# Wider opening loads, later second halves and a new order in a fused attention and gated FFN kernel

## The chip, the cores and the metric

The kernel runs on one core of one Trainium2 chip. The metric is device time in microseconds (us) from launch to end. Every change is judged by the median of several runs of the kernel before and after on the same chip.

## The reference

One input `x` of 2048 rows and 512 columns (bf16) goes through two branches, and a gate per row mixes them:

```python
def _A_ref(x, wqkv, wo):                       # sliding window attention
    B, S, D = x.shape
    H = 32; Dh = D // H; W = 256               # 32 heads of 16
    q, k, v = ...(x @ wqkv)...
    scores = einsum("bhqd,bhkd->bhqk", q, k) * (Dh ** -0.5)
    mask = (idx[:, None] - idx[None, :] >= 0) & (idx[:, None] - idx[None, :] < W)
    p = softmax(where(mask, scores, -1e9))
    return einsum("bhqk,bhkd->bhqd", p, v).reshape(B, S, D) @ wo

def _B_ref(x, w1, w3, w2):                     # gated FFN, F = 1376
    return (silu(x @ w1) * (x @ w3)) @ w2

g = sigmoid((x * gate_w).sum(-1, keepdims=True))
return g * a + (1 - g) * b
```

## The kernel before, in words

**Tiling.** The 2048 rows are 16 tiles of 128, or 4 blocks of 512 (`tq`, `tcb`). The 512 columns are 4 groups of 128 (`c`, called channel groups here: 8 heads each). `xT` holds x turned (columns on the partitions). F is cut into 11 pieces `f`: ten of 128 and a last one of 96.

**Attention.** For each `c` and `tq`, `projections` makes K and Q by matmuls of 512 columns (L449) and V (L507); for the very first block K and Q are made in two halves of 256 columns, so that the first half needs only the first two row tiles. `main_batch` (L568) makes scores of one row tile for eight heads into the only PSUM buffer `su`, ScalarE (ACT) takes the exponential of 128x2048 (L572, 1.88 us), and GpSimd (POOL) masks it (L577, L582). `edge_batch` does the same for the window's edges (L618, L622, L635). `pv` multiplies by V (L708), and VectorE (DVE) turns, normalises and turns back into `OT` (L732 to L742). `output` multiplies `OT` by `wo` (L926).

**FFN.** For each block of 512 rows: matmuls with w1 and w3 (L844), tanh on ACT (L854), two products on DVE (L858, L864) into `hT`; the 32 odd columns of F go apart (`tail_columns`, L795) through `hb` and a transposing DMA into `hX` (L819). Then W2 (L897) for four row tiles. For the last row tile (15) W2 runs in three column parts at the very end (`last_part`, L953).

**The order.** All of this is put in a list of jobs by `Plan.add`, with a duration, what it waits for, and a due time. `Plan.emit` walks through a model of the run and writes one fixed order for all engines: the engine that can start first is served, and among its jobs that can start then the one with the earliest due time. Due times come from the constants `K`: attention's batches are spread evenly over `TA` us from `T0` (`at(c, t)`), FFN's work over `TF0` to `TF1`, and offsets (`PV`, `EDGE`, `V`, `LEAD`, `QLEAD`, `PE`, `O0` to `O3` and others) move single kinds. A job of TensorE has a form ("full", "row" for scores, "column" for PV); `ADJ` is taken from the due time of a score or PV job when another has just run, `SEP` is added to a PV job's when a full one has. The order is made when the program is built, so it is fixed; each engine works through its own list and waits by semaphores.

**Loads.** `opening` runs ahead of the plan: a memset, `WARM` small matmuls on zeros (L308), and the first loads, issued on the queues of SP (SyncE) and ACT. x's first four row tiles come as they are into `xs` and are turned by TensorE (L386); the other blocks come by transposing DMA (`turn_x`). `load_w` loads columns f0 to f1 of a weight for all 512 rows, so a row of one transfer is 2 x (f1 - f0) bytes. Weights of Q, K and V come first for group 0 alone; the rest comes by `late`: a small memset on POOL (L361) into the target, planned for a given time, and behind it the load on SP, which must wait for the memset. The lists `landed` tell the plan when each opening load is supposed to be there.

The parts that the change touches, with the line numbers of the profile:

Of the kernel before, what the change touches and what calls it, by code (L numbers as in the profile page):

```python
# [15 lines left out]
P = 128  # L16
# [135 lines left out]
def kernel(  # L152
# [29 lines left out]
    VW = DH + 1  # L182
    HALF = (0, 1, 2, 3, 4)
    SCALE = float(DH) ** -0.5
    WARM = 27

    pp = ctx.enter_context(tc.tile_pool(name="pp", bufs=1))
    ps = ctx.enter_context(tc.tile_pool(name="ps", bufs=1, space=bass.MemoryType.PSUM))
# [41 lines left out]
    su = ps.tile([P, 4, 512], F32, name="su")  # L230
    ch = [ps.tile([P, 512], F32, name=f"ch_{i}") for i in range(4)]

    K = {"T0": 5.549, "TA": 217.14, "TF0": -5.82, "TF1": 246.66, "PV": 1.255, "EDGE": -3.585, "HOLD": -3.739, "LEAD": -1.218, "QLEAD": -5.876, "V": 9.009, "O0": 3.298, "O1": 2.321, "O2": 0.732, "O3": 31.615, "FE": 11.808, "PE": -3.471, "VE": -0.148, "MK": 8.747, "UP": 10.86, "_km": 1.0, "_lo": 1.0, "LE": 6.107, "ADJ": 9.389, "SEP": -24.496, "BE": 0.712, "END": 5.72}
    plan = Plan({"su": 1, "ch": 4, "Em": len(Em), "Ee": len(Ee), "tt": 2, "h1": 2,
                 "tn": len(tn), "ot": len(ot), "hT": 1},
                K["ADJ"], K["SEP"])
# [45 lines left out]
    def load_x(m0, m1, eng):  # L282
        eng.dma_start(out=xs[:, m0:m1, :],
                          in_=x2d[P * m0:P * m1, :].rearrange("(m p) d -> p m d", p=P))
# [6 lines left out]
    def load_w(dst, src, f0, f1, both=False):  # L291

        rows = src[:, f0:f1].rearrange("(c p) f -> p c f", p=P)
        for eng, c0, c1 in ((nc.sync, 0, 2), (nc.scalar, 2, 4)) if both else ((nc.sync, 0, 4),):
            eng.dma_start(out=dst[:, c0:c1, f0:f1], in_=rows[:, c0:c1, :])
# [14 lines left out]
    def opening():  # L310
        nc.vector.memset(warm[:], 0.0)
        constants()
        warm_up(WARM)

        nc.scalar.activation(out=gt[:, 0:4], in_=warm[:, 0:4], func=ACT.Tanh)
        load_x(0, 1, nc.sync)
        load_x(1, 2, nc.scalar)
        load_w(wqkv_sb, A_wqkv, D, D + P, True)
        load_x(2, 3, nc.sync)
        load_x(3, 4, nc.scalar)  # L320
        nc.scalar.dma_start(out=gwr[:], in_=gate_w.rearrange("(c p) -> c p", p=P))
        load_w(wqkv_sb, A_wqkv, 0, P)
        load_w(w1_sb, B_w1, 0, P)
        load_w(w3_sb, B_w3, 0, P)
        load_w(wqkv_sb, A_wqkv, 2 * D, 2 * D + P)
        load_w(w1_sb, B_w1, P, 2 * P)
        load_w(w3_sb, B_w3, P, 2 * P)
        turn_x(1)
        load_w(w1_sb, B_w1, 2 * P, 6 * P)
        load_w(w3_sb, B_w3, 2 * P, 6 * P)  # L330
        turn_x(2, 0, 1)
        load_w(w1_sb, B_w1, 6 * P, F)
        turn_x(2, 1, 2)
        load_w(w3_sb, B_w3, 6 * P, F)
        turn_x(2, 2, 4)
        constants2()
        constants3()
        constants4()
        constants5()
# [3 lines left out]
    PV_DUE, EDGE_DUE, HOLD = K["PV"], K["EDGE"], K["HOLD"]  # L343
    OUT_DUE = [T0 + TA + K["O%d" % i] for i in range(4)]
    step = TA / (NDC * NT)
    landed = {"x": [3.25, 3.4, 4.5, 4.6, 12.2, 21.5], "w13": [6.3, 6.8, 7.9, 8.4, 15.4, 18.7],
              "qkv": [4.1, 5.4, 7.4], "gw": 7.5}

    def at(c, t):
        return T0 + step * (c * NT + t)  # L350
# [17 lines left out]
        return done  # L368

    def rest(b):  # L370
        return lambda: load_w(wqkv_sb, A_wqkv, b * D + P, (b + 1) * D)

    x_in.append(late(25.8, xT[0:1, 0, 3 * 512:3 * 512 + 2], [lambda c=c: turn_x(3, c, c + 1) for c in range(NDC)], 1.27, 2.5))
    for b, us in ((1, 44.6), (0, 46.4), (2, 48.2)):
        qkv_in.append(late(us, wqkv_sb[0:1, 0, b * D + P:b * D + P + 2], [rest(b)]))

    xt_ready = [[] for _ in range(NTC)]
    for m in range(4):
        job = Job()

        def half_bank(job=job):
            return ch[job.at["ch"]][:].bitcast(BF16)[:, 0:D].rearrange("p (c t) -> p c t", c=NDC)

        def tr(m=m, half_bank=half_bank):
            for c in range(NDC):
                nc.tensor.transpose(out=half_bank()[:, c, :], in_=xs[:, m, c * P:(c + 1) * P], identity=ident[:])  # L386

        def ev(m=m, half_bank=half_bank):
            dst = xT[:, :, m * P:(m + 1) * P]
            if m != 2:  # L390
                nc.vector.tensor_copy(out=dst, in_=half_bank())
            else:
                nc.scalar.copy(out=dst, in_=half_bank())

        a = add("PE", 0.36 if m < 2 else 0.23, tr, [x_in[m]], (0.0, 0.1, 1.5, 1.6)[m], take=[(job, "ch")])
        b = add("DVE" if m != 2 else "ACT", 0.43 if m != 2 else 0.6, ev, [a], 0.1 * m,
                free=[(job, "ch")])
        xt_ready[0].append(b)
    for tq in range(1, NTC):
        xt_ready[tq].append(x_in[tq + 3])  # L400

    add("PE", 0.33, lambda: warm_up(4), [x_in[1]], 0.5)


    gjob = Job()
# [26 lines left out]
    def projections(c, tq):  # L432
# [8 lines left out]
            qwar += [far_ops[(c - 1, h)] for h in range(max(0, tq - 1), tq + 1)]  # L441
        else:
            vwar, qwar = [], []
        src = list(xt_ready[tq]) + [qkv_in[5 if c else 2]]

        def chain(job, col, lo, hi, t0=0, t1=512):
            pst = ch[job.at["ch"]]
# [16 lines left out]

        def by_half(src):
            return src.rearrange("p (k h t) -> p k h t", h=2, t=KB)
        a = project(kj, D, [qkv_in[3 if c else 0]], due, [(kj, "ch")])
        def kev_a():
            nc.vector.tensor_scalar_mul(out=kv0, in0=by_half(ch[kj.at["ch"]][:]), scalar1=rowsA[:, 0:1])

# [15 lines left out]
        def qev():  # L486
            copy = nc.scalar.copy if qeng == "ACT" else nc.vector.tensor_copy
            copy(out=qT[:, tq * 512:(tq + 1) * 512], in_=ch[qj.at["ch"]][:])
        a = project(qj, 0, [qkv_in[4 if c else 1]] + qwar, qdue, [(qj, "ch")])
        q_ready[(c, tq)] = add(qeng, 0.69, qev, [a], qdue, free=[(qj, "ch")])  # L490


# [275 lines left out]
    for dst, c0, src in ((wA, 0, w1_sb[:, :, F0:F0 + FA]), (wA, FA, w3_sb[:, :, F0:F0 + FA]),  # L768
                         (wB, 0, w1_sb[:, :, F0 + FA:F]), (wB, FB, w3_sb[:, :, F0 + FA:F])):
        def w_copy(dst=dst, c0=c0, src=src):  # L770
            nc.gpsimd.tensor_copy(out=dst[:, :, c0:c0 + src.shape[2]], in_=src)

        w_ab.append(add("POOL", 0.4, w_copy, [w13_in[5]], 22.0))

    b_ready = {}
    w2_in = []
# [4 lines left out]
    for tcb in range(NTC):  # L781
# [52 lines left out]
        for f in range(NFC):  # L834
            if f == NFC - 4:
                turned = tail_columns()
            joint = f == NFC - 1
            due = ffn_due(0.87 if joint else 1.73)
            job = Job()
            up = job if joint else Job()  # L840

            def half(job, w, lo, hi, f=f, joint=joint, tcb=tcb):
                for dc in range(lo, hi):
                    nc.tensor.matmul(ch[job.at["ch"]][:],  # L844
                                     lhsT=wA[:, dc, :] if joint else w[:, dc, f * P:(f + 1) * P],
                                     rhs=xT[:, dc, tcb * 512:(tcb + 1) * 512],
                                     start=(dc == 0), stop=(dc == NDC - 1))


            rg = slice(0, FA if joint else P)  # L850
            ru = slice(FA if joint else 0, P)

            def th(job=job, rg=rg):
                nc.scalar.activation(out=tt[job.at["tt"]][rg, :], in_=ch[job.at["ch"]][rg, :],  # L854
                                     func=ACT.Tanh, scale=0.5)

            def m1(job=job, rg=rg, ru=ru):
                nc.vector.scalar_tensor_tensor(out=h1[job.at["h1"]][ru, :], in0=tt[job.at["tt"]][rg, :],  # L858
                                               scalar=1.0, in1=ch[job.at["ch"]][rg, :],
                                               op0=ALU.add, op1=ALU.mult)  # L860

            def m2(job=job, up=up, rg=rg, ru=ru, f=f, joint=joint, tcb=tcb):
                dst = hX[rg, tcb % 2, :] if joint else hT[:, f, :]
                nc.vector.scalar_tensor_tensor(out=dst, in0=h1[job.at["h1"]][ru, :],  # L864
                                               scalar=0.5, in1=ch[up.at["ch"]][ru, :],
                                               op0=ALU.mult, op1=ALU.mult)

            win = [w13_in[2 * f if f < 2 else 4 if f < 6 else 5]]
            win3 = [w13_in[2 * f + 1]] if f < 2 else []
            a = plan.pieces(HALF, 0.2155, lambda lo, hi, half=half, job=job: half(job, w1_sb, lo, hi),  # L870
                            xt_ready[tcb] + win + last_up + (w_ab if joint else []), due, [(job, "ch")])
            b = a
            if not joint:
                b = plan.pieces(HALF, 0.2155, lambda lo, hi, half=half, up=up: half(up, w3_sb, lo, hi),
                                [a] + win3, due + K["UP"], [(up, "ch")])
            last_up[:] = [b]
            t_ = add("ACT", 0.595, th, [a], due - K["FE"], take=[(job, "tt")])
            s1 = add("DVE", 0.68, m1, [t_], due - K["FE"], take=[(job, "h1")], free=[(job, "tt")] + ([] if joint else [(job, "ch")]))
            s2 = add("DVE", 0.682, m2, [s1, b] + (turned if joint else []), due - K["FE"],
                     take=[(hj, "hT")] if f == 0 else [], free=[(up, "ch"), (job, "h1")])  # L880
            if f:
                s2.deps.append(hs[0])
            hs.append(s2)
# [121 lines left out]
```

## Time and profile before

| | |
|---|---|
| median of 3 runs | 238.26 us (237.95 to 238.62) |
| profiled execution, its own time | 238.49 us |
| its span (first to last instruction) | 236.8 us |
| granted TensorE clock, mean | 0.998 |
| TensorE (PE) busy | 225.3 us, 95% |
| weight loads (PEld) busy | 118.0 us, 50% |
| VectorE (DVE) busy | 185.0 us, 78% |
| ScalarE (ACT) busy | 178.0 us, 75% |
| GpSimd (POOL) busy | 154.2 us, 65% |
| DMA | 11.59 MB, 21741 packets, of which 13672 under 512 bytes |

The profile is of one execution. Times in it count from the first instruction's span; PE's busy time is the union of its matmuls, whose ends are modelled. "SPq" and "ACTq" are the queues' issues of DMA, "us to landing" runs from the issue to the semaphore that says that the data is there. An entry in brackets tells how long an engine stood idle before a group and what ended that.

### The profile page before, as it was taken

What the parts mean: (1) busy time and instruction counts of PE and PEld (TensorE: products, weight loads), DVE (VectorE), ACT (ScalarE), POOL (GpSimd) and SP (SyncE); (2) the same over time, 40 slices, a digit from 0 to 9 for tenths busy, and PEclk for the clock granted to TensorE, in tenths of its full rate; (3) what the DMA queues carried; (4) which work ended last, traced back from release to release, by engine and by line L of the source; (5) the groups of instructions that cost most, each with busy time, mean ns of one, the idle gap of its engine ahead of it and who ended that gap; (6) DMA issues with size and microseconds to landing.
All of it is one profiled execution on the core that took longest, in us unless ns stands there. A gap on an engine that the chain in (4) does not pass through costs nothing.

```text
span 236.8 us, 8534 instructions
## 1 busy us (share of the span) xinstructions
PE 225.3 (95%) x3712; PEld 118.0 (50%) x3758; DVE 185.0 (78%) x323; ACT 178.0 (75%) x153; POOL 154.2 (65%) x261
## 2 busy tenths in 40 slices
PE   6998999999999999999999999999999999999994
PEld 5652544635454545445454545445464545435453
DVE  5573998966799898777797978878599788968874
ACT  2578799776889899876789889786879997878301
POOL 7167956986776757467677667764859779474400
PEclk9999999999999999999999999999999999999999
DMA  6789047243000000000000003000000001120202
GB/s 161 144 201 304 11 83 188 84 111 91 3 3 0 13 14 0 6 0 4 3 3 3 4 6 88 23 0 3 4 3 3 4 11 36 65 95 6 69 22 89
DMA packets 21741, 11.59 MB, mean 49 GB/s; under 512 B 13672, under 2 KB 21704, under 8 KB 21704
## 3 DMA queue, kind: packets, MB, share of 16 engines
q1 hardware_dynamic: 20992, 10.69, 17.8%
q8 instruction: 29, 0.48, 0.9%
q10 hardware_dynamic: 712, 0.36, 0.5%
q14 instruction: 8, 0.07, 0.1%
HBM read 6.85 MB, written 2.10 MB: 38 GB/s over the span
## 4 chain that ended last, share of the span: by engine, by line
PE 85%; POOL 5%; DVE 4%; issue 3%; DMA 2%; ACT 0%; SPq 0%; DVEq 0%; POOLq 0%
PE ch L844 27%; PE ch L897 15%; PE ch L449 11%; PE ch L708 9%; PE su L568 8%; PE ch L926 6%; PE ch L507 6%; PE su L618 2%; DMA xs<-in_A_x_dram 2%; POOL vs L525 1%; POOL Ee L635 1%; PE ch L795 1%; POOL Em L577 1%; POOL Em L582 1%; DVE tn L732 1%
## 5 line engine op out<-in xcount | busy, mean ns | idle before, releaser
L572 ACT ACTIVATE Em<-su 128x2048 bf16<-128x2048 f32 x60 | 112.6, 1877 | 28.3 <-PE su L568 22.3
L844 PE MATMUL ch<-xT,w_sb 128*128 128x512 bf16 x297 | 77.5, 380 | 2.8 <-ACT tt L854 0.9
L577 POOL TENSOR_SCALAR_AFFINE_SELECT Em<-Em 64x512 bf16<-64x512 bf16 x60 | 42.3, 705 | 39.0 <-ACT Em L572 29.8
L635 POOL TENSOR_SCALAR_AFFINE_SELECT Ee<-Ee 64x1024 bf16<-64x1024 bf16 x32 | 36.7, 1148 | 14.9 <-ACT Ee L622 13.7
L844 PEld LDWEIGHTS <-w_sb 128*128 128x128 bf16 x320 | 28.1, 98 | 35.2 <-issue 6.8
L858 DVE SCALAR_TENSOR_TENSOR h<-tt,ch 128x512 bf16<-128x512 bf16 (+1 forms) x44 | 29.7, 678 | 12.6 <-ACT tt L854 12.3
L582 POOL TENSOR_SCALAR_AFFINE_SELECT Em<-Em 64x512 bf16<-64x512 bf16 x56 | 36.5, 652 | 3.4
L525 POOL COPY vs<-vs 64x256 bf16<-64x256 bf16 (+1 forms) x80 | 32.5, 407 | 8.8 <-DVE vs L520 5.7
L897 PE MATMUL ch<-w_sb,hT 128*128 128x512 bf16 x142 | 36.8, 380 | 0.5 <-issue 0.3
L622 ACT ACTIVATE Ee<-su 128x2048 bf16<-128x2048 f32 x16 | 30.0, 1876 | 5.7 <-PE su L618 4.3
L449 PE MATMUL ch<-xT,wqkv_sb 128*128 128x512 bf16 (+1 forms) x125 | 32.2, 366 | 1.3 <-issue 0.5
L864 DVE SCALAR_TENSOR_TENSOR hT<-h,ch 128x512 bf16<-128x512 bf16 x40 | 27.3, 681 | 4.0 <-PE ch L844 2.0
L854 ACT ACTIVATE tt<-ch 128x512 bf16<-128x512 f32 (+1 forms) x44 | 26.0, 595 | 2.5 <-PE ch L844 2.4
L708 PEld LDWEIGHTS <-vs 128*17 128x17 bf16 x1664 | 20.4, 92 | 7.0 <-issue 5.9
L708 PE MATMUL ch<-Em,vs 128*17 128x256 bf16 (+2 forms) x672 | 22.5, 242 | 0.3
L708 PE MATMUL ch<-Ee,vs 128*17 128x64 bf16 x992 | 22.1, 193 | 0.0
L897 PEld LDWEIGHTS <-hT 128*128 128x128 bf16 x150 | 13.2, 98 | 16.1 <-issue 2.3
L449 PEld LDWEIGHTS <-wqkv_sb 128*128 128x128 bf16 x136 | 12.3, 97 | 13.5 <-issue 3.1
L901 DVE TENSOR_SCALAR bsb<-ch,omg 128x512 bf16<-128x512 f32 x15 | 11.1, 744 | 10.0 <-PE ch L897 9.9
L568 PE MATMUL su<-qT,kz 32*128 32x256 bf16 x240 | 17.3, 278 | 0.7 <-ACT Em L572 0.2
L507 PEld LDWEIGHTS <-xT 128*128 128x128 bf16 x256 | 15.7, 98 | 4.4 <-issue 0.8
L568 PE MATMUL su<-qT,k 32*128 32x256 bf16 x240 | 16.7, 268 | 0.0
(84 smaller groups left out, 248.6 us busy)
## 6 DMA issues: line engine op xcount, KB each, us to landing
out_dram<-ot SPq DMA_DIRECT2D x15, 128.0 KB, 1.7
w_sb<-in_B_w_dram SPq DMA_DIRECT2D x2, 608.0 KB, 6.0
w_sb<-in_B_w_dram SPq DMA_DIRECT2D x3, 384.0 KB, 3.7
wqkv_sb<-in_A_wqkv_dram SPq DMA_DIRECT2D x3, 384.0 KB, 3.3
w_sb<-in_B_w_dram SPq DMA_DIRECT2D x2, 512.0 KB, 5.6
w_sb<-in_B_w_dram SPq DMA_DIRECT2D x5, 128.0 KB, 3.4
wo_sb<-in_A_wo_dram SPq DMA_DIRECT2D x4, 128.0 KB, 2.4
xs<-in_A_x_dram SPq DMA_DIRECT2D x2, 128.0 KB, 3.1
```

The lines of the kernel that those rows point to most:

```text
L449: nc.tensor.matmul(pst[:, t0:t1], lhsT=wqkv_sb[:, dc, col + c * P:col + (c + 1) * P], rhs=xT[:, dc, tq * 512 + t0:tq * 512 + t1], start=(d ...
L507: nc.tensor.matmul(pst[:, mm * w:(mm + 1) * w], lhsT=xT[:, dc, m * P:(m + 1) * P], rhs=rhs, start=(dc == 0), stop=(dc == NDC - 1))
L525: nc.gpsimd.tensor_copy(out=v_of(to, base, a), in_=v_of(half, 0, a))
L568: nc.tensor.matmul(su[:, s, a * 256:(a + 1) * 256], lhsT=head_keys(r, t, a), rhs=qT[r, q0:q0 + 256], start=True, stop=True)
L572: nc.scalar.activation(out=Em[job.at["Em"]][:], in_=su[:].rearrange("p s (a q) -> p s a q", a=2), func=ACT.Exp, scale=SCALE)
L577: nc.gpsimd.affine_select(out=e, in_=e, pattern=[[0, 8], [1, KB]], compare_op=ALU.is_ge, fill=0.0, base=0, channel_multiplier=-1)
L582: nc.gpsimd.affine_select(out=e, in_=e, pattern=[[0, 8], [-1, KB]], compare_op=ALU.is_ge, fill=0.0, base=-1, channel_multiplier=1)
L622: nc.scalar.activation(out=Ee[ej.at["Ee"]][:].rearrange("p s t k q -> p s (t k q)"), in_=su[:], func=ACT.Exp, scale=SCALE)
L635: nc.gpsimd.affine_select(out=e, in_=e, pattern=[[0, 4], [0, 4], [1, KB]], compare_op=ALU.is_ge, fill=0.0, base=0, channel_multiplier=-1)
L708: nc.tensor.matmul(po[32 * s:32 * s + VW, lo - 512 * w:hi - 512 * w], lhsT=vs[:, i, a * VW:(a + 1) * VW], rhs=mov, start=(n == 0), stop=(n ...
L844: nc.tensor.matmul(ch[job.at["ch"]][:], lhsT=wA[:, dc, :] if joint else w[:, dc, f * P:(f + 1) * P], rhs=xT[:, dc, tcb * 512:(tcb + 1) * 512],
L897: nc.tensor.matmul(bps[:], lhsT=ht[:, mm * P:(mm + 1) * P], rhs=w2_sb[0:fs, f, :], start=(f == 0), stop=(f == NFC - 1))
```

## The change

The opening loads x in two transfers of 256 KB (one on SP, one on ACT) instead of four of 128 KB. Each of Q, K, V, w1 and w3 comes with 256 columns in the opening instead of 128 (K in two halves on two queues), so their rows are 512 bytes instead of 256 and w1 and w3 no longer come in two pieces of 128 columns. The Q, K, V weights of channel groups 0 and 1 are now in the opening; the three memsets with the loads of the rest (now 256 columns each, groups 2 and 3) are planned for 66.5 to 70.5 us instead of 44.6 to 48.2. There are 25 instead of 27 warm-up matmuls, and 2 instead of 4 in the gap behind the first transposes. The supposed landings are changed with this, the transposes of row tiles 2 and 3 have other due times, and every constant of `K` is another, so the order of the whole run is made anew.

```diff
-    WARM = 27
+    WARM = 25
-    K = {"T0": 5.549, "TA": 217.14, "TF0": -5.82, "TF1": 246.66, "PV": 1.255, "EDGE": -3.585, "HOLD": -3.739, "LEAD": -1.218, "QLEAD": -5.876, "V": 9.009, "O0": 3.298, "O1": 2.321, "O2": 0.732, "O3": 31.615, "FE": 11.808, "PE": -3.471, "VE": -0.148, "MK": 8.747, "UP": 10.86, "_km": 1.0, "_lo": 1.0, "LE": 6.107, "ADJ": 9.389, "SEP": -24.496, "BE": 0.712, "END": 5.72}
+    K = {"T0": 4.657, "TA": 189.716, "TF0": -4.346, "TF1": 204.201, "PV": -9.134, "EDGE": -4.469, "HOLD": -13.78, "LEAD": -3.361, "QLEAD": -2.817, "V": 6.621, "O0": 4.337, "O1": 5.832, "O2": 1.283, "O3": 68.417, "FE": 10.765, "PE": 1.959, "VE": -6.383, "MK": 9.325, "UP": 8.628, "_km": 1.0, "_lo": 1.0, "LE": 5.885, "ADJ": 3.219, "SEP": -14.444, "BE": -0.49, "END": 8.139}
...
-        load_x(0, 1, nc.sync)
-        load_x(1, 2, nc.scalar)
-        load_w(wqkv_sb, A_wqkv, D, D + P, True)
-        load_x(2, 3, nc.sync)
-        load_x(3, 4, nc.scalar)
+        load_x(0, 2, nc.sync)
+        load_x(2, 4, nc.scalar)
+        load_w(wqkv_sb, A_wqkv, D, D + 2 * P, True)
         nc.scalar.dma_start(out=gwr[:], in_=gate_w.rearrange("(c p) -> c p", p=P))
-        load_w(wqkv_sb, A_wqkv, 0, P)
-        load_w(w1_sb, B_w1, 0, P)
-        load_w(w3_sb, B_w3, 0, P)
-        load_w(wqkv_sb, A_wqkv, 2 * D, 2 * D + P)
-        load_w(w1_sb, B_w1, P, 2 * P)
-        load_w(w3_sb, B_w3, P, 2 * P)
+        load_w(wqkv_sb, A_wqkv, 0, 2 * P)
+        load_w(w1_sb, B_w1, 0, 2 * P)
+        load_w(w3_sb, B_w3, 0, 2 * P)
+        load_w(wqkv_sb, A_wqkv, 2 * D, 2 * D + 2 * P)
         turn_x(1)
         load_w(w1_sb, B_w1, 2 * P, 6 * P)
         load_w(w3_sb, B_w3, 2 * P, 6 * P)
...
-    landed = {"x": [3.25, 3.4, 4.5, 4.6, 12.2, 21.5], "w13": [6.3, 6.8, 7.9, 8.4, 15.4, 18.7],
-              "qkv": [4.1, 5.4, 7.4], "gw": 7.5}
+    landed = {"x": [3.75, 3.75, 4.45, 4.45, 12.2, 21.5], "w13": [7.2, 8.1, 15.4, 18.7],
+              "qkv": [5.25, 6.2, 8.8], "gw": 8.0}
...
     def rest(b):
-        return lambda: load_w(wqkv_sb, A_wqkv, b * D + P, (b + 1) * D)
+        return lambda: load_w(wqkv_sb, A_wqkv, b * D + 2 * P, (b + 1) * D)
-    for b, us in ((1, 44.6), (0, 46.4), (2, 48.2)):
-        qkv_in.append(late(us, wqkv_sb[0:1, 0, b * D + P:b * D + P + 2], [rest(b)]))
+    for b, us in ((1, 66.5), (0, 68.5), (2, 70.5)):
+        qkv_in.append(late(us, wqkv_sb[0:1, 0, b * D + 2 * P:b * D + 2 * P + 2], [rest(b)]))
...
-        a = add("PE", 0.36 if m < 2 else 0.23, tr, [x_in[m]], (0.0, 0.1, 1.5, 1.6)[m], take=[(job, "ch")])
+        a = add("PE", 0.36, tr, [x_in[m]], 0.1 * m, take=[(job, "ch")])
...
-    add("PE", 0.33, lambda: warm_up(4), [x_in[1]], 0.5)
+    add("PE", 0.11, lambda: warm_up(2), [x_in[1]], 0.5)
...
-        a = project(kj, D, [qkv_in[3 if c else 0]], due, [(kj, "ch")])
+        a = project(kj, D, [qkv_in[0 if c < 2 else 3]], due, [(kj, "ch")])
...
-            win = [w13_in[2 * f if f < 2 else 4 if f < 6 else 5]]
-            win3 = [w13_in[2 * f + 1]] if f < 2 else []
+            win = [w13_in[0 if f < 2 else 2 if f < 6 else 3]]
+            win3 = [w13_in[1]] if f < 2 else []
```

The lines that make Q and V wait for their weights change like those of K.

More of the change, by code (lines that the diff above doesn't have):

```diff
@@ L443, in projections @@
             vwar, qwar = [], []
-        src = list(xt_ready[tq]) + [qkv_in[5 if c else 2]]
+        src = list(xt_ready[tq]) + [qkv_in[2 if c < 2 else 5]]
         def chain(job, col, lo, hi, t0=0, t1=512):
@@ L488, in qev @@
             copy(out=qT[:, tq * 512:(tq + 1) * 512], in_=ch[qj.at["ch"]][:])
-        a = project(qj, 0, [qkv_in[4 if c else 1]] + qwar, qdue, [(qj, "ch")])
+        a = project(qj, 0, [qkv_in[1 if c < 2 else 4]] + qwar, qdue, [(qj, "ch")])
         q_ready[(c, tq)] = add(qeng, 0.69, qev, [a], qdue, free=[(qj, "ch")])
@@ L771, in w_copy @@
             nc.gpsimd.tensor_copy(out=dst[:, :, c0:c0 + src.shape[2]], in_=src)
-        w_ab.append(add("POOL", 0.4, w_copy, [w13_in[5]], 22.0))
+        w_ab.append(add("POOL", 0.4, w_copy, [w13_in[3]], 22.0))
     b_ready = {}
```

## The prediction

> **What bounds the kernel now.** I read four views in this order: the page's busy shares, the stretches of the windows view, TensorE's own timeline in the opening, and the DMA issues with their landings.
>
> ```profile
> PE 225.3 (95%) x3712; PEld 118.0 (50%) x3758; DVE 185.0 (78%) x323; ACT 178.0 (75%) x153; POOL 154.2 (65%) x261
> ```
>
> TensorE (PE) is busy 225.3 of 236.8 us, the next engine 78%. So time is won only where PE stands idle, 11.5 us in all, and the windows say where (columns: stretch, its length, then busy time and instructions of PE, weight loads, DVE, ACT, POOL; at the end the granted clock, DMA share and GB/s).
>
> ```profile
> 0.00:4.00 4.00, 2.93 (x31) 2.94 (x31) 2.37 (x6) 1.49 (x2) 2.93 (x19) 1.00 0.39 112
> 4.00:6.00 2.00, 0.80 (x15) 0.63 (x13) 0.76 (x2) 0.00 (x0) 1.84 (x6) 1.00 1.03 262
> 17.00:19.20 2.20, 1.09 (x7) 0.42 (x6) 0.13 (x1) 2.20 (x3) 1.97 (x7) 1.00 1.22 250
> 24.00:60.00 36.00, 35.01 (x630) 17.85 (x636) 29.40 (x59) 28.59 (x26) 27.48 (x54) 1.00 0.39 93
> 60.00:226.00 166.00, 162.51 (x2826) 83.12 (x2861) 136.01 (x223) 134.30 (x107) 112.10 (x164) 1.00 0.06 17
> 226.00:232.50 6.50, 6.50 (x41) 3.55 (x38) 5.22 (x8) 0.02 (x1) 0.00 (x0) 1.00 0.09 29
> ```
>
> PE loses 1.07 us before its first instruction, 1.2 us in 4 to 6, 1.1 us in 17 to 19.2, but 1.0 + 3.5 = 4.5 us in the 202 us from 24 to 226, and nothing from there to 232.5. The last 4.3 us are the fixed end (last evictions and stores). The two holes in the opening have names:
>
> ```profile
> 5.86 0.64 PE L386 MATMUL ch<-ident,xs 128*128 128x128 bf16 x8 [1.20 <-DMA xs<-in_A_x_dram]
> 19.08 1.04 PE L844 MATMUL ch<-xT,w_sb 128*128 128x512 bf16 x4 [0.95 <-ACT tt L854]
> ```
>
> The first waits for rows 2 and 3 of x. The second is put down to ACT, but the list of waits has a weight load of L844 that waited 1.4 us for a DMA of w_sb, so it is the third weight w3, columns 256 to 767, that was late. Both hang on SP's queue of issues:
>
> ```profile
> 5.83 0.37 SPq L295 DMA_DIRECT2D wqkv_sb<-in_A_wqkv_dram  x1
> 6.41 0.92 SPq L295 DMA_DIRECT2D w_sb<-in_B_w_dram  x2
> 7.37 5.11 SPq L288 DMA_TRANSPOSE xT<-in_A_x_dram  x4
> 12.53 1.42 SPq L295 DMA_DIRECT2D w_sb<-in_B_w_dram  x2
> ```
>
> Before 5.83 SP stood 2.0 us, "SPq L295 <- DMA xs" in its waits: with several transfers in flight the next issue waits for an older landing. Then come two small loads, four transposing loads at 1.28 us each, and only at 12.53 the large w1 and w3 pieces. The second of these was issued near 13.15 and took 5.6 us to land: 18.75, and PE resumes at 19.08.
>
> **The change, part by part.** *Bytes and rate.* Before, x (512 KB) and seven 128 KB weight pieces, 1408 KB, with weight rows of 256 bytes; after, x and five pieces of 256 KB, 1792 KB, with rows of 512. No row of this trace has 512-byte rows; these bound them:
>
> ```profile
> 7.50:8.00 0.50, 0.50 (x7) 0.44 (x6) 0.15 (x1) 0.00 (x0) 0.00 (x0) 1.00 1.17 230
> 50.00:50.50 0.50, 0.50 (x4) 0.26 (x3) 0.26 (x1) 0.50 (x1) 0.50 (x1) 1.00 0.99 333
> 20.00:20.50 0.50, 0.50 (x10) 0.23 (x10) 0.34 (x1) 0.00 (x0) 0.50 (x1) 1.00 1.08 382
> ```
>
> At 7.5 (256-byte rows) a full DMA share moves 230/1.17 = 197 GB/s; at 50 (rows of 768 bytes, the late QKV pieces) 333/0.99 = 336; at 20 (1,024 and 1,216) 354. A piece of 256 KB therefore takes between 0.78 us (336) and 1.33 us (197). I take 0.87 us (300), nearer to 768 bytes because the rows at 50 are also an uneven cut of a wide matrix.
>
> *Arrival.* The first bytes flow at 2.05. At 344 GB/s (window 2.5 to 3) x takes 1.5 us, with 0.35 us to its landing 3.9; the bad end is x2's landing before (640 KB ahead of it, landed 5.8), scaled to 512 KB: 5.05. I take 4.3 for x. K, 768 KB in all, lies between 3.55 + 0.78 + 0.35 = 4.7 and (5.8 - 2.05) x 768/640 + 2.05 = 6.55; the sum of GB/s over the half-microsecond windows of before reaches 768 KB at 5.25, so I take 5.4. Q then follows at 6.3, w1 at 7.1, w3 at 8.0, V at 8.9.
>
> *PE in the opening.* Before: transposes of rows 2 and 3 at 5.86, first K matmul 6.34, first FFN matmul (L844) 8.30. After: 25 warm-ups end near 3.8, all 16 transposes run from 4.3 to 5.6 (two groups of 0.64), K and Q then take the same 1.75 us as before: FFN from about 7.45, w1 being there. That is 0.85 us earlier; I count **-0.8 us**. With the bad end (K at 6.55, w1 with 1.33 us pieces at 9.2) it is +0.9, with the good end -1.3. Two and two fewer warm-ups lie in time in which PE waits for x in any case: 0. Later landings of V are covered: L507 used V at 11.97 before, and 8.9 leaves 3 us (10.7 at 1.33 us a piece still leaves 1).
>
> *SP's queue.* After, SP issues x, K, Q, w1, w3, V, then the four transposes: two pieces fewer. The ninth transfer in flight is V, which waits for the landing of x (4.3) instead of 5.83, and the transposes start near 4.8 rather than 7.37. Each may wait once more for an older landing (K 5.4, Q 6.3), so they end near 10 instead of 12.48, and w1 and w3 (columns 256 to 767) are issued 2.5 us earlier. With the same 5.6 us to landing w3 is there at 16.3; PE, 0.8 us ahead, wants it at 18.13 - 0.8 = 17.3. The hole of 0.95 closes: **-0.9 us**, between 0 (transposes that are slowed by 384 KB more in front of them) and -1.0. What comes next is the copies of wA on POOL, which waited 0.8 us for w3's last columns; these come earlier too.
>
> *The rest of Q, K, V.* Three memsets of 0.09 us on POOL and three loads on SP move from 48.2-53 to some 70-78 (planned for 66.5 to 70.5; before, the first ran at 48.1 for a planned 44.6); each load shrinks from 384 to 256 KB. SP waits for POOL there; queued behind are the transposes of hX of the second token block, which ran at 80.29 before, in a stretch in which SP otherwise has nothing to do from 53 to 80. Channel group 1 now has its weights from the opening; group 2 is due at 4.657 + 94.9 = 99.5 us, and these loads took at most 3.8 us to land: 20 us of cover. Cost 0; if a rest came after 100 us, PE would have FFN work to put in its place.
>
> *The order.* Every constant of K changes, but many cancel. What ranks a PV job while PE is in full shape is PV + SEP: 1.255 - 24.496 = -23.2 before, -9.134 - 14.444 = -23.6 after. V against its batch is V - LEAD: 10.2 before, 10.0 after. HOLD is negative in both, so it picks nothing. What does shift: PV's first DVE step, due at PV - PE = +4.7 before, -11.1 after, goes ahead of FFN's steps; ADJ 9.4 to 3.2 keeps fewer attention jobs side by side (PV's own lead takes its place: PV - ADJ is -8.1 and -12.4); and the FFN runs further ahead. Its share done when attention's due time ends is (222.69 + 5.82)/252.48 = 0.905 before and (194.37 + 4.35)/208.55 = 0.953 after. From 24 to 226 only 4.5 us of idle are left, so a new order can gain perhaps a third, 1.5 us, and can lose as much as is there, 4.5. I take **+0.3 us**, near zero since the effective ranks are near each other.
>
> Sum: -0.8 - 0.9 + 0.3 = -1.4 us. The profiled execution took 238.49 us, 1.69 beyond its span, and the median of the runs is 238.26, so the sum stands against 0.2 us of scatter: 238.3 - 1.4 = **236.9 us**.
>
> **Rivals.** *The end is uncovered (slower).* After the last PV (L708, to 225.2) DVE needs from 225.26 to 228.43 to bring OT for the last output; PE fills that with ten L897 matmuls (2.1 us) and the first L953 group (1.2 us). Before it, between the last scores (219.44) and PV (223.76), L926 and L897 fill another 3.9 us. When attention's last batch (3,14) is due, FFN has 12.2% of 112.6 us left before, 13.7 us, but 7.6%, 8.5 us, after. If the W2 products of rows 12 to 14 are used up by then, the first hole opens by 2.1 us, and the second by up to 3.9: a price from 2.1 to 6.0, I take 3.0, giving 239.9. It decides where fewer than some 2 us of L897 stand behind the last L708. For it speaks that the window at 226 has no idle at all, so this end can only get worse; against, that twelve outputs (10 us) are due as late as before relative to that batch.
>
> *No gain in the opening (no change).* Pieces land as late as x2 did, or the array's clock is not up: 25 cold warm-ups took 314 ns each, 219 ns from the first transposes on; per matmul (2.93 - 0.314)/26 = 0.10 us against (0.61 - 0.219)/7 = 0.056. Were K and Q to run at the slow pace, their 1.75 us would become 3.1, and -0.8 + 1.35 - 0.9 + 0.3 is about 0: 238.2. [...]
>
> *A better order on top (faster still).* A third of the 4.5 us goes: 235.2.
>
> **How the numbers follow.** Forecast 0.40, better order 0.09, no gain 0.14, uncovered end 0.37. About 0.3% (0.7 us) is what a measurement of this kernel can tell from no change: faster 0.49, same 0.14, slower 0.37. The likeliest case alone spans 235.8 to 237.5; the range from 235.0 to 241.0 takes in the better order and the end uncovered by up to 4 us.
>
> **What would show it.** Right: first L844 at 7.2 to 7.8; transposes issued before 5.5 and ended by 10.5; no L844 wait over 0.3 us near 17 to 19; idle from 24 to the last PV within 4 to 5.5 us; at least 2 us of L897 behind the last L708. Wrong: first L844 after 8.3, a new wait for DMA between 8 and 24, weight loads of L449 in group 2 that wait for wqkv_sb, or PE idle between the last L708 and the last L926.

## The result, and the profile after

The changed kernel took 236.56 us (median of 6 runs) against 238.3 us before; the ratio is 0.992 with a 95% interval from 0.9894 to 0.9945, a gain of 0.8%. The forecast was 236.9 us, faster. One of the six executions, the profiled one, took 573.19 us, with 814 ns instead of 380 for a matmul of 512 columns; the ratio leaves it out, and without it the median is 236.08 us. The profile after shown here is therefore that of experiment e1, the same kernel run again (ratio 0.9904, from 0.989 to 0.9919; span 234.2 us). Behind the opening's loads, the lines of the changed kernel are 4 lower than before (L844 is L840, L449 is L445); the experiments have offsets of their own (the same matmuls are L452 in e3, e6 and e7).

The windows view of e1, four of the stretches of the prediction (stretch, length, busy time and count for PE, weight loads, DVE, ACT, POOL, then clock, DMA share, GB/s):

```profile
4.00:6.00 2.00, 2.00 (x22) 1.83 (x19) 1.22 (x3) 0.59 (x1) 1.85 (x6) 1.00 1.07 300
17.00:19.20 2.20, 2.20 (x12) 0.86 (x9) 0.61 (x3) 1.96 (x2) 1.98 (x6) 1.00 0.99 306
24.00:60.00 36.00, 33.88 (x626) 17.45 (x633) 28.69 (x58) 28.64 (x29) 25.89 (x48) 1.00 0.24 60
60.00:226.00 166.00, 161.87 (x2832) 83.72 (x2864) 135.95 (x222) 132.91 (x105) 112.23 (x166) 1.00 0.07 20
```

Both holes of the opening are gone: PE is busy 2.00 of 2.00 us and 2.20 of 2.20. TensorE's timeline in e1 shows how:

```profile
1.07 2.85 PE L308 MATMUL su<-warm 128*128 128x128 bf16 x25 [1.07 <-DVE warm L311]
3.71 1.88 PE L382 MATMUL ch<-ident,xs 128*128 128x128 bf16 x16
5.54 2.05 PE L445 MATMUL ch<-xT,wqkv_sb 128*128 128x256 bf16 x16
7.64 2.54 PE L840 MATMUL ch<-xT,w_sb 128*128 128x512 bf16 x11
...
12.24 1.24 PE L445 MATMUL ch<-xT,wqkv_sb 128*128 128x512 bf16 x5
```

Behind the first warm-up no group is preceded by a wait, and the first FFN matmul stands at 7.64 instead of 8.30. Keep the group of five L445 at 12.24 in mind: four of them are Q's or K's usual chain, and one is not. SP's queue in e1:

```profile
3.60 0.37 SPq L295 DMA_DIRECT2D wqkv_sb<-in_A_wqkv_dram  x1
4.78 5.42 SPq L288 DMA_TRANSPOSE xT<-in_A_x_dram  x4
10.25 1.13 SPq L295 DMA_DIRECT2D w_sb<-in_B_w_dram  x2
```

V is issued at 3.60 instead of 5.83, the transposing loads from 4.78 instead of 7.37, the large w1 and w3 pieces at 10.25 instead of 12.53.

### The profile page after: what moved, and what is told of

Same layout as the page of the kernel before. It is cut to its first block, busy times and chain, and to the rows that moved or that the text cites. A ratio compares the mean times of both kernels' runs of the same rounds, so it can differ in the third digit from the quotient of the medians.

```text
span 571.4 us, 8525 instructions
## 1 busy us (share of the span) xinstructions
PE 551.0 (96%) x3709; PEld 214.4 (38%) x3754; DVE 187.7 (33%) x323; ACT 183.4 (32%) x153; POOL 152.4 (27%) x261
## 4 chain that ended last, share of the span: by engine, by line
PE 96%; issue 3%; DVE 0%; ACT 0%; ACTq 0%
PE ch L840 33%; PE ch L893 17%; PE ch L445 13%; PE ch L704 9%; PE ch L503 7%; PE ch L922 7%; PE su L564 6%; PE su L614 2%; PE ch L949 1%; PE ch L791 1%; PE su L308 1%; PE ch L382 0%; DVE tn L728 0%; ACT tt L850 0%; DVE ot L953 0%
## 5 line engine op out<-in xcount | busy, mean ns | idle before, releaser
L840 PE MATMUL ch<-xT,w_sb 128*128 128x512 bf16 x298 | 189.3, 814 | 6.5 <-issue 6.5
L893 PE MATMUL ch<-w_sb,hT 128*128 128x512 bf16 x141 | 90.6, 821 | 2.7 <-issue 2.7
L840 PEld LDWEIGHTS <-w_sb 128*128 128x128 bf16 x320 | 46.8, 156 | 104.4 <-issue 103.3
L445 PE MATMUL ch<-xT,wqkv_sb 128*128 128x512 bf16 (+1 forms) x127 | 76.9, 792 | 2.8 <-issue 2.2
L704 PEld LDWEIGHTS <-vs 128*17 128x17 bf16 x1664 | 45.6, 140 | 23.9 <-issue 15.0
L704 PE MATMUL ch<-Em,vs 128*17 128x256 bf16 (+2 forms) x672 | 52.5, 398 | 0.0
L704 PE MATMUL ch<-Ee,vs 128*17 128x64 bf16 x992 | 51.3, 293 | 0.0
L503 PEld LDWEIGHTS <-xT 128*128 128x128 bf16 x256 | 34.9, 168 | 18.5 <-issue 16.2
L922 PE MATMUL ch<-wo_sb,OT 128*128 128x512 bf16 x61 | 38.2, 829 | 1.0 <-issue 1.0
L445 PEld LDWEIGHTS <-wqkv_sb 128*128 128x128 bf16 x136 | 20.4, 158 | 42.4 <-issue 40.6
L564 PE MATMUL su<-qT,k 32*128 32x256 bf16 x240 | 32.4, 520 | 0.0
```

Of the source, the lines that this page charges most:

```text
L445: nc.tensor.matmul(pst[:, t0:t1], lhsT=wqkv_sb[:, dc, col + c * P:col + (c + 1) * P], rhs=xT[:, dc, tq * 512 + t0:tq * 512 + t1], start=(d ...
L503: nc.tensor.matmul(pst[:, mm * w:(mm + 1) * w], lhsT=xT[:, dc, m * P:(m + 1) * P], rhs=rhs, start=(dc == 0), stop=(dc == NDC - 1))
L564: nc.tensor.matmul(su[:, s, a * 256:(a + 1) * 256], lhsT=head_keys(r, t, a), rhs=qT[r, q0:q0 + 256], start=True, stop=True)
L704: nc.tensor.matmul(po[32 * s:32 * s + VW, lo - 512 * w:hi - 512 * w], lhsT=vs[:, i, a * VW:(a + 1) * VW], rhs=mov, start=(n == 0), stop=(n ...
L840: nc.tensor.matmul(ch[job.at["ch"]][:], lhsT=wA[:, dc, :] if joint else w[:, dc, f * P:(f + 1) * P], rhs=xT[:, dc, tcb * 512:(tcb + 1) * 512],
L893: nc.tensor.matmul(bps[:], lhsT=ht[:, mm * P:(mm + 1) * P], rhs=w2_sb[0:fs, f, :], start=(f == 0), stop=(f == NFC - 1))
```

## The experiments

Each kernel was timed in five rounds against the kernel before on the same chip, in three groups of four (e1 to e4 and e9 to e12 on one chip, e5 to e8 on another); ratios are to that. "New loads" are those of the change; "old order" is the plan of before.

**e1, the changed kernel again.** No edit.

> The changed kernel once more, for a profile in which TensorE runs at its usual pace. Theory A (the loads bring the gain, the new order about nothing): 236.4 us, first FFN matmul near 7.45, no wait for DMA of over 0.3 us between 8 and 24. Theory B (the new order brings the gain, the loads nothing): 236.4 as well, but the first FFN matmul near 8.3 and less idle of TensorE than 4.5 us between 24 and 226.

Measured: 236.16 us, 0.9904. Shown above: the first FFN matmul at 7.64 (A), no wait between 8 and 24 beyond 0.16 us. It doesn't decide by itself.

**e2, new loads, old order.** The opening's loads and `rest` are the new ones; on PE, DVE and POOL the instructions stand exactly as before.

```diff
 (kernel before)
-        load_x(0, 1, nc.sync)
...
+        load_x(0, 2, nc.sync)
+        load_x(2, 4, nc.scalar)
+        load_w(wqkv_sb, A_wqkv, D, D + 2 * P, True)
...
-        return lambda: load_w(wqkv_sb, A_wqkv, b * D + P, (b + 1) * D)
+        return lambda: load_w(wqkv_sb, A_wqkv, b * D + 2 * P, (b + 1) * D)
```

> The new opening loads (and the rest of the weights shrunk to groups 2 and 3, at the old times) under the order of before, instruction for instruction. Theory A: 0.8 us in the opening and 0.9 us at 17 to 19 are saved, so 238.3 - 1.7 = 236.6 us. Theory B: within 0.4 us of before, 238.3.

Measured: 237.49 us, 0.9964 (0.9948 to 0.998), 0.9 us. That is half of what theory A expected. In e2's timeline the opening has no wait, but no gain either:

```profile
1.07 3.06 PE L308 MATMUL su<-warm 128*128 128x128 bf16 x27 [1.07 <-DVE warm L311]
3.92 1.06 PE L386 MATMUL ch<-ident,xs 128*128 128x128 bf16 x8
4.78 0.63 PE L308 MATMUL su<-warm 128*128 128x128 bf16 x4
5.21 1.06 PE L386 MATMUL ch<-ident,xs 128*128 128x128 bf16 x8
...
8.26 2.54 PE L844 MATMUL ch<-xT,w_sb 128*128 128x512 bf16 x11
```

x is there in time, but 31 warm-ups, 16 transposes and the first K and Q run back to back and fill the time up to 8.26 (8.30 before). In this execution each eight transposes took 1.06 us, against 0.61 and 0.64 in the profile of before: TensorE was still at its slow pace. What e2 gains is a part of the hole at 17 to 19: PE is busy 1.91 of 2.20 us there instead of 1.09, and the wait that is left, 0.55 us up to 19.46, ends behind the stretch.

**e3, old loads, new order.** The pieces of before; the halves for channel group 1 are added behind the opening's last load.

```diff
 (changed kernel, opening loads of before)
         turn_x(2, 2, 4)
+        load_w(wqkv_sb, A_wqkv, D + P, D + 2 * P)
+        load_w(wqkv_sb, A_wqkv, P, 2 * P)
+        load_w(wqkv_sb, A_wqkv, 2 * D + P, 2 * D + 2 * P)
```

> The new order, instruction for instruction, over the opening loads of before (128 KB pieces, rows of 256 bytes); the pieces for channel group 1 come at the end of the opening. Theory A: the order alone costs 0.3 us, 238.6; at most what the plan's shorter waits lose on top, 239.2. Theory B: 236.4 us.

Measured: 249.4 us, 1.046 (1.0446 to 1.0474). Theory A missed by 11 us and theory B by 13, and the timeline of e3 tells why:

```profile
11.67 1.08 PE L510 MATMUL ch<-wv,xT 128*128 128x129 bf16 x16
25.18 2.31 PE L452 MATMUL ch<-xT,wqkv_sb 128*128 128x512 bf16 x5 [12.42 <-DMA wqkv_sb<-in_A_wqkv_dram]
```

At 12.8 PE reaches the same five matmuls as e1 at 12.24 and stands for 12.42 us until the first added load, issued at 21.22, has landed. Behind this wait the five matmuls took 2.31 us instead of 1.24, and the granted clock was 0.75 from 17 to 19.2 and 0.50 from 19.2 to 24. The first of the five is a matmul of channel group 1: only group 1's weights land then. In the written order its chain (one matmul ahead of the projections of the second block, three more near 16, at 15.84 and 16.71 in e8) has a due time of 55.45, 40 us later: the plan used it as filler because it believed those weights to be there. Before, group 1's weights came from 48 us on, so no such filler existed. So the new order can't be had over loads that bring group 1's weights that late; the two parts don't add.

**e4, warm-ups back.** `WARM = 27` and `warm_up(4)` in the changed kernel.

> The changed kernel with 27 and 4 warm-up matmuls again instead of 25 and 2, all else alike. If TensorE waits for x behind the warm-ups (theory A): 236.4 us, within 0.2. If x is there first, the two cold matmuls cost 0.2 us and the two warm ones 0.1: 236.7. If the fewer warm-ups leave the clock low for the first projections, this one is faster by up to 1.3 us: 235.1.

Measured: 235.79 us, 0.989 (0.9875 to 0.9905), the intervals of e1 and e4 overlap, so none of the three cases is shown. The first FFN matmul came 0.29 us later (7.93), as four more matmuls make it, but in e1's profile PE lost 0.40 us near 36 to a wait for the last block of x that e4's doesn't have. The extra warm-ups cost 0.29 us at the opening and nothing measurable at the end.

**e5, group 1 not before 50 us.** All loads as in the change.

```diff
+    g1_in = arrive(50.0)
...
-        a = project(kj, D, [qkv_in[0 if c < 2 else 3]], due, [(kj, "ch")])
+        a = project(kj, D, [g1_in if c == 1 else qkv_in[0 if c < 2 else 3]], due, [(kj, "ch")])
 (and the same for Q and V)
```

> The changed kernel, all loads alike, but the plan may not use the weights of channel group 1 before 50 us. Theory C (the new order gains early because projections of group 1 stand in for waits between 12 and 24 us, which the early weights allow): that gain, 1.2 us over the first 20 us of work, goes, 237.4 us. Theory D (the order gains by its constants wherever it runs): within 0.4 us of 236.2.

Measured: 242.77 us, 1.0172 (1.0155 to 1.0188), 6.5 us slower than the change, far more than either. The constraint gives another order everywhere. Part of it is what C foresaw: waits of 0.66 us near 16 and 1.22 near 25. A large part is the end:

```profile
230.41 1.03 PE L923 MATMUL ch<-wo_sb,OT 128*128 128x512 bf16 x4
232.28 1.02 PE L923 MATMUL ch<-wo_sb,OT 128*128 128x512 bf16 x4 [0.84 <-DVE ot L927]
234.15 1.02 PE L923 MATMUL ch<-wo_sb,OT 128*128 128x512 bf16 x4 [0.84 <-DVE ot L927]
236.01 1.02 PE L923 MATMUL ch<-wo_sb,OT 128*128 128x512 bf16 x4 [0.84 <-DVE ot L927]
```

Here the last outputs go one by one, each waiting for DVE: 2.5 us of uncovered end. So e5 shows the rival of the prediction, the uncovered end, at work in another order, and it doesn't isolate C.

**e6, narrow pieces, and e7, half pieces.** Both keep the order of the change and the same bytes ahead of the transposing loads. e6 uses the 128 KB pieces and 256-byte rows of before, with group 1's pieces right behind; e7 keeps 512-byte rows but cuts the 256 KB pieces into two of 128 KB (K came in two halves already). Ahead of the transposing loads SP then issues 11 transfers in e7 and 12 in e6, against 6 in e1.

```diff
 (e7)
-        load_w(w1_sb, B_w1, 0, 2 * P)
+        load_h(w1_sb, B_w1, 0, 2 * P)     # two transfers: rows 0-255, rows 256-511
```

> The changed kernel and its order, with the same bytes ahead of the first transposing load, but all in 128 KB pieces with weight rows of 256 bytes. If the row's length sets the rate (197 against some 300 GB/s, the prediction's step), 1280 KB of weights take 2.2 us longer, the transposes and what follows them slip by about that, and TensorE waits near 12: 238.4 us. If neither rows nor pieces matter: 236.2.

> The changed kernel and its order, rows of 512 bytes as there, but 128 KB pieces (x by single row tiles, the weights by halves of their 512 rows). If the row's length alone matters: 236.2 us. If the number of issues on SP does (5 more at about 0.45 us, and the limit on transfers in flight): the transposes start 1 to 2.3 us later and the time is 236.8 to 238.5.

Measured: e6 239.06 us, 1.0038 (1.0015 to 1.0061); e7 238.21 us, 0.9986 (0.9964 to 1.0007). Against the ratio of the changed kernel (0.9904 in e1; 0.9905 in e8, of the same group as e6 and e7), cutting the pieces costs 0.8% (2.0 us), and what e6 does beyond that another 0.5% (1.2 us): shorter rows, one more transfer on SP and another order of the pieces, which no run here takes apart. The transposing loads start at 4.78 in e1, 7.83 in e7 and 9.18 in e6. In both e6 and e7 the first FFN matmul comes at 8.50, and PE then waits for the second block of x. From e7:

```profile
6.96 1.70 PE L452 MATMUL ch<-xT,wqkv_sb 128*128 128x256 bf16 x14 [1.08 <-DMA wqkv_sb<-in_A_wqkv_dram]
15.96 0.38 PE L452 MATMUL ch<-xT,wqkv_sb 128*128 128x512 bf16 x1 [1.63 <-DMA xT<-in_A_x_dram]
```

So the number of transfers was worth more than the length of their rows, under this order.

**e8, the rest at the old times.** `(1, 44.6), (0, 46.4), (2, 48.2)`; PE, DVE and SP stand in the same order, POOL's three memsets stand earlier.

> The changed kernel with the three memsets and the loads of the rest planned at 44.6, 46.4 and 48.2 us as before; TensorE's order is the same. The prediction took their move for free: 236.2, within 0.2 us. If the memsets or loads at 66 to 70 collide with something: faster by the size of that.

Measured: 236.39 us, 0.9905 (0.9889 to 0.9921), as the change. Moving the rest costs nothing that this can tell.

**e9, e2 with four warm-ups fewer.** `WARM = 25` and `warm_up(2)`, nothing else.

> The new loads under the old order (as in e2_loads), with four warm-up matmuls fewer (25 and 2); every engine's order is otherwise that of before. In the profile of e2_loads TensorE runs through from the first warm-up to the first FFN matmul at 8.26 with no wait for x or K, at 0.107 us a cold matmul. If so, four fewer give 0.43 us: 237.0 to 237.1. If K's landing stands behind them (the prediction: warm-ups lie in a wait), nothing: 237.5.

Measured: 237.27 us, 0.9935 (0.9909 to 0.9961); the medians differ by 0.2 us from e2, the ratios by 0.7, so the size is not settled. In the profile the first FFN matmul moved from 8.26 to 7.99, and 0.17 us before it are a wait for w1: the warm-ups had stood in the way, and behind them is the DMA. Then, in this execution, the old order still meets the hole, now for w3:

```profile
13.21 0.29 PE L568 MATMUL su<-qT,kz 32*128 32x256 bf16 x4 [0.23 <-ACT Em L572]
18.41 1.04 PE L844 MATMUL ch<-xT,w_sb 128*128 128x512 bf16 x4 [0.73 <-DMA w_sb<-in_B_w_dram]
```

**e10, four matmuls left out.** `chain` returns at once for Q of group 1, first block.

> The changed kernel without the four matmuls (0.86 us of TensorE's time) of Q for channel group 1, first block, which its order has at 12.2 and between 15.5 and 16.6; they are left out, so this Q is not computed. Theory C (they stand in what would be waits): 236.2 us, no gain. Theory D (TensorE would have had other work there): 235.3.

Measured: 236.47 us, 0.9905 (0.9879 to 0.9931). It missed its aim: K and Q of that block have the same due time, and the order's early filler is K. PE's timeline between 12 and 24 is unchanged, the group of five included; the Q left out stands later, since it must wait for group 0's scores to be done with `qT`. In e8, with all matmuls, it is part of the seven L445 from 60.29 on and PE reaches the scores at 62.55 without a wait; without it PE waits 0.67 us for ACT and reaches the same scores at 62.56. So this Q stood in what would have been a wait too, but late. What the early filler is worth alone stays open.

**e11 and e12, two edits on top.** In e11 the last block of x is no longer held back by a memset on POOL; in e12 the last columns of w1 and w3 are also issued ahead of the third block of x. PE's order is that of the change.

```diff
 (e11)
-        return add("POOL", 0.08, lambda: nc.gpsimd.memset(ap, 0.0), [arrive(us)], us)
+        return add("POOL", 0.08, (lambda: None) if us == 25.8 else lambda: nc.gpsimd.memset(ap, 0.0), [arrive(us)], us)
 (e12, also)
-        turn_x(2, 0, 1)
         load_w(w1_sb, B_w1, 6 * P, F)
-        turn_x(2, 1, 2)
         load_w(w3_sb, B_w3, 6 * P, F)
-        turn_x(2, 2, 4)
+        turn_x(2)
```

> The changed kernel without the memset on GpSimd that holds back the last block of x (its four transposing loads then go out right behind the others on SP, near 20 instead of near 30 us). In the profiles TensorE waited 0.4 to 0.6 us near 36 for this block. If that wait is on the path to the end: 235.8 us. If other waits take its place or the load disturbs the last w1 and w3 pieces: 236.2 or more.

> As e11_x3, and the last columns of w1 and w3 are issued ahead of the third block of x. TensorE waited 0.4 to 0.6 us near 25.5 for GpSimd's copies of w1 and w3's last columns, which wait for these loads. If the copies come 2 us earlier: another 0.4, 235.4 us. If the third block of x is then late: slower than e11_x3 by up to 1 us.

Measured: e11 235.79 us, 0.9874 (0.9848 to 0.9901); e12 235.56 us, 0.9862 (0.9835 to 0.9888). The wait for x near 36 is gone in both profiles; POOL's copies still hold PE up for 0.60 and 0.46 us near 25.6, so the second edit did little. Both came out near what was expected. e11's interval overlaps e1's; e12's, 1.4% below the kernel before, ends 0.0002 below it, in another group: the best medians seen, but not clearly better than the change.

## Why the prediction was right, point by point

**The total: right, in part by luck.** The forecast had -1.7 us for the loads and +0.3 for the order, -1.4 in all; the ratio of the result, 0.992, makes -1.9, that of e1 -2.3. With the warm-ups held at 27 and 4, the loads alone gave -0.9 (e2) and the order on top of them -1.8 (e4 against e2: 0.989 against 0.9964, in one group on one chip). Two errors of opposite sign cancelled.

**Arrivals: right.** Forecast and landing in e1 (issue plus time to landing): x 4.3 against 0.82 + 2.8 = 3.6 on SP and 1.05 + 3.3 = 4.35 on ACT; K 5.4 against 1.50 + 3.9 = 5.4; w1 7.1 against 2.34 + 4.8 = 7.1; V 8.9 against 3.60 + 5.2 = 8.8. The rate behind them was somewhat overrated: in e1 a full DMA share moved 300/1.07 = 280 GB/s from 4 to 6 us, mostly at 512-byte rows, where 300 was taken.

**SP's queue: right on the issues, too early on the landing.** Start 4.78 for 4.8, end 10.20 for 10, w1 and w3 issued 2.3 us earlier for 2.5; the hole of 0.95 us is closed in e1. But w3 took 6.5 us to land instead of 5.6, and came at 17.38, not 16.3; PE's weight load for it starts at 17.42. The hole closed with nothing to spare: in e9 w3 came at 18.36, and 0.73 us of wait were left. The account of the cause was also one-sided. It set the gain down to bytes and rate, and counted two pieces fewer where SP issues 6 instead of 9; of the 3.2 us between e1 and e6, 2.0 come with the number of transfers alone (e7). 256-byte rows did move less (197 GB/s at a full DMA share in the profile of before) than e1's mix, mostly of 512-byte rows (280), and that less than rows of 1,024 bytes and more (354, before), but the rows were the smaller part here: 1.2 us go with all that e6 does beyond e7.

**PE in the opening: right in sum, wrong in its terms.** -0.8 was forecast and 7.64 against 8.30 is -0.66. K and Q were put at "the same 1.75 us as before", but in the profile of before it is 1.96 from the first K matmul to the first FFN matmul (6.34 to 8.30), and 2.10 in e1. And the step "two and two fewer warm-ups lie in time in which PE waits for x in any case: 0" failed in e1: the first rows of x came at 3.6, the warm-ups ran to 3.9, and the last rows came at 4.35 while PE turned the first, so nothing was left to wait for. The loads alone (e2) gave 0.04 us up to the first FFN matmul; with fewer warm-ups (e9) 0.31, in spite of the wait for w1. The other 0.35 us to e1's 7.64 lie between single profiles and are not shown to come from the order: the first FFN matmul of the changed kernel stands at 7.72 in e8 and at 7.46 in e11.

**The order: the wrong sign.** The term +0.3, for which the prediction allowed a gain of 1.5 and a loss of 4.5, was mis-sized. With 27 and 4 warm-ups the order alone gives 1.8 us (e2 to e4); with 25 and 2 it gives 0.7 (e9's 0.9935 to e1's 0.9904), and there the intervals overlap. The fewer warm-ups seem to gain 0.7 us under the old order and to cost 0.3 under the new one, neither clear of the noise. The comparison of ranks in the middle of the run was no help: the waits that went lay ahead of 24 us. Two profiles in which no matmul's record is missing (of which more below), first e9 (old order), then e8 (the change's order), show it:

```profile
8.00:24.00 16.00, 14.87 (x146) 7.32 (x147) 9.68 (x25) 13.04 (x17) 9.57 (x20) 1.00 1.02 211
8.00:24.00 16.00, 15.95 (x153) 7.51 (x152) 10.81 (x27) 12.48 (x16) 10.17 (x24) 1.00 0.95 211
```

From 8 to 24 us PE stands idle for 1.13 us in e9 and for 0.05 in e8. That group 1's projections, which the plan now has ready there, are what fills this time is the likely reading; e5 and e10 were to show it and did not.

**The 4.5 us of idle were mostly not there.** The prediction bounded the order's gain by PE's idle time from 24 to 226, and named 4 to 5.5 us of it up to the last PV as a sign of being right. e1's windows add up to 2.12 + 4.13 = 6.3 us, outside that, but the measure itself was no good. The page of before shows why:

```profile
L844 PE MATMUL ch<-xT,w_sb 128*128 128x512 bf16 x297 | 77.5, 380 | 2.8 <-ACT tt L854 0.9
...
L844 PEld LDWEIGHTS <-w_sb 128*128 128x128 bf16 x320 | 28.1, 98 | 35.2 <-issue 6.8
```

320 weight loads and 297 matmuls: 23 records are missing, and the holes that they leave read as idle, most of them released by "issue". e1's profile lacks records too (298 of 320); those of e8 and e9 have all 320. First e9, whose order on PE is that of before, then e8:

```profile
24.00:60.00 36.00, 35.56 (x637) 17.70 (x636) 29.40 (x59) 28.47 (x27) 27.45 (x54) 1.00 0.36 82
60.00:226.00 166.00, 165.59 (x2862) 83.16 (x2861) 136.03 (x222) 133.84 (x107) 111.61 (x163) 1.00 0.06 18
...
24.00:60.00 36.00, 35.00 (x611) 17.20 (x612) 28.56 (x58) 28.46 (x28) 25.79 (x50) 1.00 0.35 82
60.00:226.00 166.00, 165.84 (x2893) 83.64 (x2893) 135.98 (x222) 133.51 (x106) 112.64 (x164) 1.00 0.05 15
```

Idle from 24 to 226 is 0.85 us in e9, where the same order showed 4.5 before, and 1.16 in e8, nearly all of it before 60. So there were no 4.5 us to win or lose there by waits.

**The rest of Q, K, V: right**, free by e8. **The uncovered end: not here.** In e1 no W2 matmul is left behind the last PV, against the sign that was named, but 19 output matmuls and 8 of the last part are, 5.2 us from 221.1 on. The mark was too narrow; the rule, that enough work must stand there, holds, and e5 shows its price. **The clock:** e1's 16 transposes took 1.88 us, 0.107 us each, where the 8 of before took 0.056 each, so TensorE was still at the slow pace; it cost less than the rival said, since K's landing at 5.4 comes right behind. When the pace changes differs between the profiles: in that of before the eight transposes from 3.83 on are quick (0.61 us), in e1 the 16 from 3.71 on are slow (1.88 us), in e2 both groups of eight, from 3.92 and from 5.21 on (1.06 us each), with 27, 25 and 27 warm-ups ahead. What sets that moment, and that it is the array's clock, no run here shows.

## What to carry to other kernels

A load and the order that was planned on it are one change: here the order was worth 0.7 to 1.8 us on top of the loads' 0.9, and over loads that came too late for it the kernel lost 11. Where one queue issues everything, count transfers before bytes: five more in front of the transposing loads pushed these by 3 us and cost 2 us in all. Before idle time of TensorE is used as a bound, compare the number of its matmuls with that of its weight loads.

## What the runs showed that was not expected

TensorE's pace in the opening differs between executions of the same instructions, and an early quick pace doesn't bring the first FFN matmul forward. In e1, e11 and e12 all 16 transposes are slow (1.88 to 1.91 us); in e8 and e10, with the same instructions up to there, they take 1.35 and 1.49. The first FFN matmul still comes at 7.64, 7.46 and 7.63 us in the first three, and at 7.72 and 7.94 in the other two. From e8:

```profile
3.71 1.35 PE L382 MATMUL ch<-ident,xs 128*128 128x128 bf16 x16
6.82 1.05 PE L445 MATMUL ch<-xT,wqkv_sb 128*128 128x256 bf16 x8 [0.63 <-DMA wqkv_sb<-in_A_wqkv_dram]
```

Where TensorE is quick early, PE waits for Q's weights: 0.63 us in e8 and 0.71 in e10. There the step of the prediction that failed in e1 holds: warm-ups lie in a wait, only for Q's weights and not for x.

The column of the granted clock doesn't tell the two paces apart: it gives 1.00 for e1 from 4 to 6 us, while the transposes start 0.107 us apart instead of 0.056. The spacing of the matmuls, or their mean duration, does.
